# An mLSTM cell with a SwiGLU block: q of the second group transposed on VectorE, with its scores, state sums and attention one place later in the order

## The chip, the core and the metric

The kernel runs on one core of a Trainium2 chip. The metric is the device time of one execution in microseconds (us). The kernel before takes 506.29 us, the median of three runs (505.01 to 506.61).

A core has five engines, each with its own queue worked in program order: TensorE (PE; its weight loads are PEld), VectorE (DVE), ScalarE (ACT), GpSimd (POOL) and SyncE (SP), which here only issues DMAs. Engines wait for each other through semaphores. SBUF is the working memory; PSUM (8 banks) takes TensorE's results.

## The reference

Two stages. The first is a recurrence over 768 time steps for 4 batches and 8 heads of 40 features each, in float32:

```python
for t in range(S):
    m_new = np.maximum(f_gate[:, :, t] + m, i_gate[:, :, t])
    f_stab = np.exp(f_gate[:, :, t] + m - m_new)
    i_stab = np.exp(i_gate[:, :, t] - m_new)
    m = m_new
    C = f_stab * C + i_stab * einsum('bhd,bhe->bhde', vt, kt)
    n = f_stab * n + i_stab * kt
    h_tilde = einsum('bhde,bhe->bhd', C, qt)
    denom = np.maximum(np.abs(einsum('bhd,bhd->bh', n, qt)), 1.0)
    y[:, :, t] = sigmoid(o_gate[:, :, t]) * h_tilde / denom
```

The second takes y as x, 3072 tokens of 320 features, through a gated block of 1536 hidden units; its weights come in as 64-bit floats:

```python
g = x @ w_gate
out = (g * sigmoid(g) * (x @ w_val)) @ w_out
```

## The kernel before

**Groups.** The 768 steps are cut into six groups of 128 steps, numbered 0 to 5. The recurrence is done in closed form: within a half group of 64 steps by a 64x64 matrix of weighted scores for each head (`scores`, `weigh`, `attend_intra`), and across halves by a state C (`add`, `next_state`, `decayed`, `attend_inter`). `gather` adds the two parts of the attention and finds the divisor, `gate` puts the divisor into the output gate (on GpSimd), and `divide` makes x of it. P is 0 or 1 and names the half of the 32 pairs of batch and head (batches 0 and 1, or 2 and 3). `seam` transposes x to xT on TensorE, for the gated block.

**The pipeline.** While a group goes through the gated block, the attention of the next one is put between the pieces of that block. Group 0 is written out most carefully, as the weights arrive with it. Its hidden layer is 12 blocks of 128 hidden units, `hidden(0, m)`: 20 matmul instructions each (L808), a silu on ScalarE (L813) and a product on VectorE (L814). Then `project_all(0)` does the output products in 12 parts, 8 instructions each (L825); part m uses hidden block m. From group 1 on `gated` (L978) and `project_seven` (L879) do the same with fewer products.

**The weights.** They come as 64-bit floats in pieces (`piece_load`), and are made into 32-bit floats block by block. `scale(j)` does two ScalarE instructions (L249, L251), `join(j)` two on VectorE (L258, L259), and `rounded(j)` one (L266) on GpSimd, or on VectorE where `V` is given; `convert(j)` is the three in a row. Blocks 0 to 11 belong to the hidden layer, 12 to 17 to the output weights, two parts each: block 12 serves parts 0 and 1. Piece 7 holds blocks 10 and 11, piece 8 blocks 12 and 13. A piece has gate columns, loaded from SP's queue, and value columns, loaded from GpSimd's (L222).

**The order around the change.** It is written out by hand. `ahead[m]` and `first` are put behind block m's matmuls but ahead of its silu; `slots[m]` comes behind its product; `after[m]` behind part m of the output products. As every engine works its queue in this order, a place in these lists sets what stands ahead of what on each engine. In the kernel before:

- Group 1's k is loaded in slot 2, its q in slot 3 (`load_all`: two DMAs, L139), its v in slot 5. k is transposed on TensorE in slot 6 (`turn_one`, L378, copies on ScalarE by L156), q likewise in the middle of block 8 (`amid`).
- The weights of the scores, w_sb, are capped in slot 6 (L570), subtracted (L559) and put through exp (L577) in slot 7. GpSimd weighs v by them there (`weigh_values`, L422).
- The scores (L411) are in slot 8, with their weighing (L418), and a memset of q_sb on GpSimd ahead of them; the decays (L454) in slot 9, the state sums (L437) and state updates (L461) in slot 10.
- The attention of group 1's half P=0 (L478, L468) is in slot 11, that of P=1 behind part 1. The two divisions (L507) are behind parts 2 and 3, each with a pad copy of x on GpSimd (L510); the two seams (L543) behind parts 4 and 5.
- Group 2's q and k go another way: `load_squares` (L395) loads 32x32 squares, with 8 DMAs for each half, and `turn_squares` transposes the squares on VectorE (L401, two instructions).

**Banks.** PSUM has two rings of four banks here. One is for hidden blocks and output products ("gen"): each block takes two banks, so that block m+2 needs block m's silu and product done. The other ("cell") is for transposes, scores, sums and attention.

Of the kernel before, what the change touches and what calls it, by code (L numbers as in the profile page):

```python
# [13 lines left out]
AF = mybir.ActivationFunctionType  # L14
# [10 lines left out]
def kernel(  # L25
# [774 lines left out]
    def hidden(g, m, first=(), amid=()):  # L800
        ps = [bank("gv_ps", "gen") for _ in range(2)]
        x = xT(g)
        for kc in range(NKC):
            if kc == 3:
                for f in amid:
                    f()
# [285 lines left out]
    def load_all(dst, a, n, eng=nc.sync):  # L1092
        for P in range(2):
# [5 lines left out]
    on_vector = (9, 10)  # L1099
    ahead = {0: [], 1: [3], 2: [4], 3: [5], 4: [6], 5: [7], 6: [8], 7: [9], 8: [10], 9: [], 10: [], 11: []}  # L1100
# [3 lines left out]
        2: [run(late_maxima), run(M_store, G), run(load_all, k_sb, k, 1)],  # L1104
        3: [run(late_decay), run(weights_load, 1), run(load_all, q_sb, q, 1)],
        4: [run(nc.scalar.activation, step1, step1, AF.Exp), run(decay_rows), run(cap_table)],
# [136 lines left out]
```

## Time and profile before

| what | value |
|---|---|
| median of three runs | 506.29 us (505.01 to 506.61) |
| time of the profiled execution | 504.85 us |
| its span | 503.1 us |
| TensorE clock granted in its span | full (1.0) |
| group 0's hidden blocks | 25.96 to 86.72 us |
| group 0's output products | 88.73 to 119.0 us |
| DMA engines, mean busy share in the first eight slices of 12.6 us | 0.9 or more in six, then 0.8 and 0.7 |

The span goes from the first to the last instruction of the profiled execution; the time has 1.75 us more around it. The page of the profile gives the busy time of each engine and the chain of waits; the timelines give single instructions with start, length, engine, line, output and inputs. Times in a timeline are from the span's start. Two rows of the same engine can overlap a little, since an instruction's length includes its latency.

### The profile page before, as it was taken

The page shows a single profiled execution, that of the slowest core. Times are in us where ns is not written, and L with a number is a line of the kernel's source. Part 1 is how long each engine was busy: PE and PEld are TensorE (multiplying, and loading weights), DVE is VectorE, ACT ScalarE, POOL GpSimd, SP SyncE. Part 2 cuts the span into 40 slices and gives each one's busy share as a digit, 9 for nine tenths or more (in the row PEclk, how much of TensorE's full clock was granted, in tenths as well). Part 3 has the DMA queues.
Part 4 walks back from the last instruction along what each step waited for, and adds up shares of the span by engine and source line. Part 5 has one row for each costly group of instructions (what it writes and reads, how often), then busy time and mean ns, then how long its engine had stood idle before and what let it go on. Part 6 is the DMA issues. An engine that isn't in the chain of part 4 may idle for free.

```text
span 503.1 us, 14945 instructions
## 1 busy us (share of the span) xinstructions
PE 498.6 (99%) x6361; PEld 424.4 (84%) x6361; DVE 333.2 (66%) x542; ACT 209.2 (42%) x406; POOL 261.1 (52%) x292
## 2 busy tenths in 40 slices
PE   9999999999999999999999999999999999999997
PEld 4856555767889899888899888899888899988897
DVE  5889869889998587578376677467468464233421
ACT  4776784476262266323247312339311330223210
POOL 3753525458876925465723357643267650176710
PEclk9999999999999999999999999999999999999999
DMA  9999998797607982404991502991101100000001
GB/s 145 194 231 244 160 210 215 169 167 115 88 3 120 157 85 52 44 3 68 165 115 45 67 3 47 161 128 27 42 3 25 32 1 27 27 1 1 1 14 39
DMA packets 184938, 43.29 MB, mean 86 GB/s; under 512 B 173128, under 2 KB 180312, under 8 KB 184360
## 3 DMA queue, kind: packets, MB, share of 16 engines
q1 hardware_dynamic: 183396, 38.00, 48.0%
q0 software_dynamic: 1344, 4.28, 3.6%
q8 instruction: 50, 0.82, 0.7%
q14 instruction: 16, 0.13, 0.1%
q10 hardware_dynamic: 132, 0.07, 0.0%
HBM read 35.68 MB, written 4.01 MB: 79 GB/s over the span
## 4 chain that ended last, share of the span: by engine, by line
PE 97%; DVE 1%; ACT 1%; issue 0%; DVEq 0%
PE gv_x L978 26%; PE o_ps L879 22%; PE gv_y L978 21%; PE gv_ps L808 10%; PE o_ps L825 5%; PE inter L468 2%; PE sp L411 2%; PE intra L478 2%; PE o_ps L884 1%; PE add L437 1%; PE tp_kq L378 1%; PE sp L641 1%; PE tp_x L543 1%; PE wps L609 1%; PE burn L587 0%; PE wps L613 0%
## 5 line engine op out<-in xcount | busy, mean ns | idle before, releaser
L978 PE MATMUL gv_x<-xT,wgv_sb 64*128 64x256 f32 x720 | 89.1, 377 | 0.0
L978 PEld LDWEIGHTS gv_x<-xT,wgv_sb 64*128 64x128 f32 x720 | 69.3, 187 | 8.1 <-issue 0.2
L879 PE MATMUL o_ps<-wo_sb,h_sb 128*128 128x160 f32 x456 | 63.9, 300 | 0.0
L879 PEld LDWEIGHTS o_ps<-wo_sb,h_sb 128*128 128x128 f32 x456 | 62.3, 190 | 1.7 <-issue 1.7
L1026 ACT ACTIVATE h_sb<-gv_x 128x256 f32<-128x256 f32 x30 | 11.5, 384 | 116.3 <-PE gv_x L978 116.3
L808 PE MATMUL gv_ps<-xT,wgv_sb 64*128 64x512 f32 x240 | 53.8, 596 | 0.0
L808 PEld LDWEIGHTS gv_ps<-xT,wgv_sb 64*128 64x128 f32 x240 | 26.7, 187 | 22.6 <-issue 14.9
L978 PE MATMUL gv_y<-xT,wgv_sb 64*128 64x256 f32 x360 | 43.9, 376 | 0.0
L978 PE MATMUL gv_y<-q_sb,wgv_sb 64*128 64x256 f32 x360 | 43.9, 376 | 0.0
L422 POOL TENSOR_TENSOR vw_sb<-v_sb,w_sb 128x656 f32<-128x656 f32 x10 | 14.6, 1464 | 51.0 <-ACT w_sb L574 38.1
L978 PEld LDWEIGHTS gv_y<-xT,wgv_sb 64*128 64x128 f32 x360 | 34.9, 187 | 4.0
L978 PEld LDWEIGHTS gv_y<-q_sb,wgv_sb 64*128 64x128 f32 x360 | 34.9, 187 | 4.0
L574 ACT ACTIVATE w_sb<-w_sb,g_T 128x64 f32<-128x64 f32 x128 | 31.0, 334 | 0.0
L978 PE MATMUL gv_x<-q_sb,sw 64*128 64x256 f32 x240 | 30.9, 376 | 0.0
L879 PE MATMUL o_ps<-wT,S 128*128 128x160 f32 x216 | 30.2, 299 | 0.0
L879 PEld LDWEIGHTS o_ps<-wT,S 128*128 128x128 f32 x216 | 29.6, 190 | 0.0
L1019 POOL TENSOR_TENSOR tmp<-tmp 128x512 f32<-128x512 f32 x15 | 20.0, 1334 | 16.8 <-DVE tmp L1018 16.8
L999 POOL TENSOR_TENSOR h_sb<-x_sb 128x512 f32<-128x512 f32 x12 | 15.7, 1306 | 24.6 <-ACT x_sb L998 24.6
L999 POOL TENSOR_TENSOR h_sb<-tmp 128x512 f32<-128x512 f32 x13 | 16.5, 1269 | 21.5 <-ACT tmp L998 21.5
L846 POOL TENSOR_TENSOR S<-h_sb 128x256 f32<-128x256 f32 x30 | 22.6, 755 | 9.2 <-DVE h_sb L999 7.3
L1018 DVE TENSOR_TENSOR x_sb<-x_sb,gv_y 128x1024 f32<-128x1024 f32 x15 | 18.1, 1205 | 13.9 <-PE gv_y L978 11.6
L825 PE MATMUL o_ps<-wo_sb,h_sb 128*128 128x320 f32 x96 | 27.1, 438 | 0.0
(238 smaller groups left out, 1004.7 us busy)
## 6 DMA issues: line engine op xcount, KB each, us to landing
w_sb<-M_dram SPq DMA_DIRECT2D x8, 512.0 KB, 6.6
raw<-in_moe_w_out_dram SPq DMA_DIRECT2D x3, 1280.0 KB, 7.1
v_sb<-in_v_dram SPq DMA_DIRECT2D x11, 320.0 KB, 9.4
o_sb<-in_o_gate_dram SPq DMA_DIRECT2D x11, 320.0 KB, 5.0
k_sb<-in_k_dram SPq DMA_DIRECT2D x9, 320.0 KB, 7.3
x_sq<-k_sb SPq DMA_DIRECT2D x64, 40.0 KB, 2.8
q_sb<-in_q_dram SPq DMA_DIRECT2D x32, 64.0 KB, 3.7
out_dram<-tmp SPq DMA_DIRECT2D x24, 80.0 KB, 1.7
```

The source lines that it names most:

```text
L411: nc.tensor.matmul(sp[two][keys(n, P, i), a, :], lhsT=kT[feats(two), P * UA + a, half(i)], rhs=qT[feats(two), P * UA + a, half(i)], start= ...
L422: eng.tensor_tensor(vw_sb[:, heads(P)], v_sb[:, heads(P)], w_sb[:, heads(P), last].to_broadcast([128, UH, D1]), op=ALU.mult)
L574: nc.scalar.activation(w_sb[:, h], w_sb[:, h], AF.Exp, bias=g_T[:, n, h:h + 1], scale=-1.0)
L808: nc.tensor.matmul(ps[i], lhsT=wgv_sb[half(i), m, kc, :], rhs=x[half(i), kc, :], start=(kc == 0), stop=(kc == NKC - 1))
L825: nc.tensor.matmul(ps[u], lhsT=hid(g, m)[:, ts(u, L)], rhs=wo_sb[:, m, :], start=(m == 0), stop=(m == NFC - 1))
L846: eng.tensor_tensor(S1[:, k], lo[:, second_half], hi[:, second_half], op=ALU.add)
L879: nc.tensor.matmul(node[x][:, i], lhsT=lhs(k)[:, ts(i, L)], rhs=rhs(k), start=start and k == 0 and i == 0, stop=stop and k == KH - 1, skip ...
L978: nc.tensor.matmul(ps[:, i, cols], lhsT=lhs(c)[half(i)], rhs=rhs(c)[half(i)], start=start and c == 0, stop=stop and c == n - 1, skip_group ...
L999: (nc.vector if k == KH - 1 else nc.gpsimd).tensor_tensor(h_sb[:, 2 * k + 1], uw[:, 0], uw[:, 1], op=ALU.mult)
L1018: nc.vector.tensor_tensor(uw, uw, y, op=ALU.add)
L1019: nc.gpsimd.tensor_tensor(uw[:, :, second_half], uw[:, :, second_half], uw[:, :, first_half], op=ALU.add)
L1026: nc.scalar.activation(h[:, first_half], x[:, 0, first_half], AF.Silu)
```

## The change

Group 1's q is loaded as squares and transposed on VectorE, like that of the later groups, so that `amid` and the transposes of q on TensorE go. Its 16 square loads are in slots 2 and 4, where two loads stood in slot 3. Piece 7's two parts are loaded in slots 3 and 5 instead of 5 and 6. The caps and one subtraction move to slot 7, the second subtraction, exp and the weighing of v to slot 8, behind the conversion of block 10, which itself moves from ahead of block 8's silu to behind its product. The scores go from slot 8 to slot 10, the sums and state updates from slot 10 to slot 11, the attention of P=0 from slot 11 to behind part 0, that of P=1 from behind part 1 to behind part 2. The first sums of weights for group 1 (`weight_sums(0, V)`) move from behind part 10 to behind part 3, the transposes of group 2's q from behind part 4 to behind part 5. The memset of q_sb goes.

```diff
-    on_vector = (9, 10)
-    ahead = {..., 7: [9], 8: [10], 9: [], 10: [], 11: []}
+    on_vector = (9,)
+    ahead = {..., 7: [9], 8: [], 9: [], 10: [], 11: []}
     slots = {
...
-        2: [run(late_maxima), run(M_store, G), run(load_all, k_sb, k, 1)],
-        3: [run(late_decay), run(weights_load, 1), run(load_all, q_sb, q, 1)],
-        4: [..., run(decay_rows), run(cap_table)],
-        5: [run(piece_load, 7, parts=GATE), run(load_all, v_sb, v, 1), run(late_turns), run(decay)],
-        6: [run(piece_load, 7, parts=VALUE)] + [run(turn_one, P, k_sb, kT, (A, A)) for P in range(2)] + [run(weights_cap, 0), run(weights_cap, 1), run(piece_load, 8)],
-        7: [run(weights_sub, 1, 0), run(weights_sub, 1, 1), run(weights_exp, 0), run(weights_exp, 1), run(weigh_values, G, 0),
-            run(weigh_values, G, 1)],
-        8: [run(nc.gpsimd.memset, q_sb, 0.0), run(do_scores, 1), run(piece_load, 9), run(load_all, o_sb, o_gate, 1),
-            run(do_weigh, 0), run(do_weigh, 1)],
-        9: [run(join, 11), run(rounded, 11, V), run(do_decayed, 2)],
-        10: [run(do_add, 1), run(do_state, 2), run(rounded, 12), run(load_squares, q_sq, q, 2, (0,))],
-        11: [run(do_intra, 1, 0), run(do_inter, 1, 0), run(do_gather, 1, 0, False), run(piece_load, 10),
+        2: [run(late_maxima), run(M_store, G), run(load_all, k_sb, k, 1), run(load_squares, q_sq, q, 1, (0,))],
+        3: [run(late_decay), run(weights_load, 1), run(piece_load, 7, parts=GATE)],
+        4: [..., run(decay_rows), run(cap_table), run(load_squares, q_sq, q, 1, (1,))],
+        5: [run(piece_load, 7, parts=VALUE), run(load_all, v_sb, v, 1), run(late_turns), run(decay)],
+        6: [run(turn_one, P, k_sb, kT, (A, A)) for P in range(2)] + [run(piece_load, 8)],
+        7: [run(weights_cap, 0), run(weights_cap, 1), run(weights_sub, 1, 0)],
+        8: [run(convert, 10, V), run(weights_sub, 1, 1), run(weights_exp, 0), run(weights_exp, 1), run(turn_squares, q_sq, qT),
+            run(weigh_values, G, 0), run(weigh_values, G, 1), run(piece_load, 9), run(load_all, o_sb, o_gate, 1)],
+        9: [run(do_decayed, 2)],
+        10: [run(do_scores, 1), run(do_weigh, 0), run(scale, 12), run(join, 12), run(do_weigh, 1), run(rounded, 12),
+             run(load_squares, q_sq, q, 2, (0,))],
+        11: [run(do_add, 1), run(do_state, 2), run(piece_load, 10),
              run(load_squares, q_sq, q, 2, (1,))],
     }
-    amid = {8: [run(turn_one, P, q_sb, qT, (A, A)) for P in range(2)]}
...
-        first += {9: [run(scale, 11)], 10: [run(scale, 12), run(join, 12)], 11: [run(convert, 13)]}.get(m, [])
-        hidden(0, m, first, amid.get(m, ()))
+        first += {9: [run(convert, 11, V)], 11: [run(convert, 13)]}.get(m, [])
+        hidden(0, m, first)
...
     after = {
-        0: [run(convert, 14), run(sig, 0), run(sig, 1), run(do_gate, 0)],
-        1: [run(do_inter, 1, 1), run(do_intra, 1, 1), run(do_gather, 1, 1), run(weights_load, 2), run(load_all, v_sb, v, 2), run(load_all, k_sb, k, 2)],
-        2: [run(do_divide, 1, 0), run(convert, 15), run(early_squares, 0)],
-        3: [run(do_divide, 1, 1), run(weights_cap, 0)],
-        4: [run(seam, 1, 0, (A, A, A, A)), run(convert, 16), run(weights_cap, 1), run(turn_squares, q_sq, qT)],
-        5: [run(seam, 1, 1, (A, A, A, A)), run(convert, 17)],
+        0: [run(do_intra, 1, 0), run(do_inter, 1, 0), run(convert, 14), run(sig, 0), run(sig, 1), run(do_gather, 1, 0)],
+        2: [run(do_divide, 1, 0), run(do_inter, 1, 1), run(do_intra, 1, 1), run(do_gather, 1, 1), run(weights_load, 2),
+            run(load_all, v_sb, v, 2), run(load_all, k_sb, k, 2), run(convert, 15), run(early_squares, 0)],
+        3: [run(do_divide, 1, 1), run(weight_sums, 0, V)],
+        4: [run(seam, 1, 0, (A, A, A, A)), run(convert, 16), run(weights_cap, 0), run(weights_cap, 1)],
+        5: [run(seam, 1, 1, (A, A, A, A)), run(convert, 17), run(turn_squares, q_sq, qT)],
...
-        10: [run(do_decayed, 4), run(weight_sums, 0, V)],
+        10: [run(do_decayed, 4)],
...
     }
```

More of the change, by code (lines that the diff above doesn't have):

```diff
@@ L798, in hid, with hidden @@
         return h_sb[:, m, :]
-    def hidden(g, m, first=(), amid=()):
+    def hidden(g, m, first=()):
         ps = [bank("gv_ps", "gen") for _ in range(2)]
@@ L803, in hidden @@
         for kc in range(NKC):
-            if kc == 3:
-                for f in amid:
-                    f()
             for i in range(2):
@@ L1096 @@
     run = lambda f, *a, **b: (lambda: f(*a, **b))
-    on_vector = (9, 10)
-    ahead = {0: [], 1: [3], 2: [4], 3: [5], 4: [6], 5: [7], 6: [8], 7: [9], 8: [10], 9: [], 10: [], 11: []}
+    on_vector = (9,)
+    ahead = {0: [], 1: [3], 2: [4], 3: [5], 4: [6], 5: [7], 6: [8], 7: [9], 8: [], 9: [], 10: [], 11: []}
     slots = {
@@ L1115 @@
-        11: [run(do_intra, 1, 0), run(do_inter, 1, 0), run(do_gather, 1, 0, False), run(piece_load, 10),
+        2: [run(late_maxima), run(M_store, G), run(load_all, k_sb, k, 1), run(load_squares, q_sq, q, 1, (0,))],
+        3: [run(late_decay), run(weights_load, 1), run(piece_load, 7, parts=GATE)],
+        4: [run(nc.scalar.activation, step1, step1, AF.Exp), run(decay_rows), run(cap_table), run(load_squares, q_sq, q, 1, (1,))],
+        5: [run(piece_load, 7, parts=VALUE), run(load_all, v_sb, v, 1), run(late_turns), run(decay)],
```

1 line of the change is left out of this document (removed).

## The prediction

> **What bounds the kernel now.** First the page: its first part says how full each engine is, its chain of waits which work ended last.
>
> ```profile
> PE 498.6 (99%) x6361; PEld 424.4 (84%) x6361; DVE 333.2 (66%) x542; ACT 209.2 (42%) x406; POOL 261.1 (52%) x292
> ...
> PE 97%; DVE 1%; ACT 1%; issue 0%; DVEq 0%
> ```
>
> TensorE carries 97% of the chain and its granted clock is full, so a microsecond taken from TensorE's queue, or a wait put into it, moves the end by itself. Next the chain between 57 and 90 us (start, length, work), where the change acts.
>
> ```profile
> 58.25 0.99 PE tp_kq L378 x32
> 59.24 4.40 PE gv_ps L808 x20
> 63.63 0.59 ACT tmp L813
> ...
> 68.20 1.06 ACT qT L156 x2
> 69.26 0.04 issue
> 69.31 2.13 PE sp L411 x126
> 71.44 8.78 PE gv_ps L808 x40
> 80.22 2.01 PE add L437 x128
> 82.23 4.49 PE gv_ps L808 x20
> ```
>
> A hidden block costs TensorE 4.4 to 4.5 us. Between 63.63 and 69.31 the chain leaves it for ScalarE's copies of q, but TensorE works on: block 8 and, within it, 32 transposes of q. Last the timelines of VectorE, GpSimd, TensorE and the DMA queue, up to the seam at 105 us.
>
> ```profile
> 72.35 3.57 POOL L422 TENSOR_TENSOR vw_sb<-v_sb,w_sb 128x656 f32<-128x656 f32 x2 [12.26 <-ACT low L251]
> 73.05 1.71 DVE L266 CUSTOM_DVE_ANT_0 wgv_sb<-wgv_sb,low 128x1280 uint16<-128x1280 uint16 x1
> ...
> 98.17 1.31 POOL L501 TENSOR_TENSOR o_sb<-o_sb,den 128x640 f32<-128x640 f32 x1 [1.68 <-DVE den L496]
> 98.29 1.54 DVE L507 TENSOR_TENSOR x_sb<-o_sb,vw_sb 128x320 f32<-128x320 f32 x1
> ...
> 102.84 1.80 POOL L1128 MEMSET raw<- 128x2048 f32 x1
> 104.59 0.28 POOL L510 COPY x_sb<-x_sb 128x128 f32<-128x128 f32 x1
> ...
> 104.94 0.84 PE L543 MATMUL tp_x<-x_sq,x_sb 64*128 64x64 f32 x20
> ```
>
> Two things are to be seen. A VectorE instruction beside a GpSimd one can take far longer than alone: 1.71 us for a rounding that takes 0.83, 1.54 for a product that takes 0.43, the latter ending 0.35 us after GpSimd's gate. And the second seam starts 0.07 us after GpSimd's pad copy ends (104.87), with no idle before it: no slack there now.
>
> **Removed from TensorE.** The 32 transposes of q are like those of k: 0.99 us. From 63.63 to 69.31 are 5.68 us; less a block (4.40 to 4.49) and 0.99, 0.20 to 0.29 us of waiting for ScalarE's copies is left, 0.25. Together **-1.24 us**, all that the change can give, as every other TensorE instruction stays. ScalarE's four copies (2.03) and GpSimd's memset of q (1.80) go too, from engines that don't set the end.
>
> **Loads.** q's two loads (issues 5.56 us together) become 16. SP's 8 issues of such squares took 5.88 and 8.78 us. SP ends group 1's k at 47.68 and now waits for M until 51.04. Behind the change 8 squares go out to some 53.6, the weights' 1.1 to 54.7, and the gate part of piece 7 (blocks 10 and 11) behind them instead of at 57.96. With its 12.7 us to landing: 67.4, up to 69.4 if its issue takes 2 us as now. ScalarE reads it at 68.7 (below), so I cost this at 0; the cover is 0.7 us past that, the slack of block 10. The other 8 squares come next (to 60.6 or 63.5, landing at most 6.6 us later, before VectorE's transposes at 72.9), then v, 0.6 to 3.5 us later than now. v's first half lands at 72.2 now: 73 to 76. Piece 8 (blocks 12 and 13) is behind v and lands at 77.3 now: 78 to 81, where ScalarE reads it from 78 on and needs it by 80; 0.
>
> **VectorE after block 8.** Now laid in order. TensorE ends block 8 at 63.63 + 4.42 = 68.05; silu (0.60) 68.65. VectorE: product 7 to 64.93, caps 2.35, one subtraction 1.2, done at 68.4; product 8 at 69.35. ScalarE's scaling of block 10 ends at 70.15, join (0.49 + 0.82) and rounding (0.83) at 71.8; block 10 starts at 72.47, 0.65 us later: 0. Second subtraction 72.95, transposes (a pair takes 2.36 at 108.64) 75.3. They have no cost of their own, but block 11 now waits for what is behind them: join 11 (two instructions), rounding 11, product 9, some 3.0 us with gaps: 78.3 if undisturbed (ScalarE's two exps, scaling 11, table load and silu 9 end at 77.4). Block 11 wants product 9's banks when block 10 (76.9) and the scores (2.06) are done: 78.95. That is 0.65 us of slack. GpSimd's two weighings (3.57) and two decays (1.71) start with v, at 73 to 76, and lie beside just these instructions; now they start at 72.35. If each VectorE instruction loses what its kind lost beside GpSimd in this trace (rounding 0.88; second join instruction 1.24 against 0.82, so 0.42; first join instruction likewise 0.4), it is 1.7 less the slack: **+1.05 us**. From both sides: 0 if the weighings lie elsewhere; 2.2 if each of the three waits behind a whole weighing (1.46) or two decays (0.72 each).
>
> The Trainium skill (SBUF — State Buffer, the summary at its end) says that a VectorE instruction in a two-port mode, or with two SBUF inputs against a GpSimd instruction that reads SBUF, blocks until the other has finished. The 1.54 us row agrees, ending 0.35 us after the gate. By that rule whole blockings are due, and the term would be nearer the 2.2 end.
>
> **Scores, sums, attention.** Scores behind block 10 leave block 11 to cover the weighing of scores (2.47), join 12 and join 13 (1.31 each) and product 11 (0.69); the sums' 2.0 us on TensorE cover the rest. The first output part wants product 11's banks: 0 to 0.7, I take **+0.2 us**. State updates and decays took 3.2 us after the sums now; block 12's rounding must precede part 0, and attention P=0 has part 0 (2.23) and the sums' own 1.0 to cover them: 0.
>
> **The seam.** Let X be the end of attention P=0 on TensorE. Gathering took 3.64 us now (88.72 to 92.36), the gate 1.3, two divisions 0.85 alone: X+5.95. Only then VectorE gathers P=1, X+9.6 (its TensorE part ends at X+6.5); now nothing but a join stands between the two gatherings. GpSimd then has the gate (1.3), rounding 15 (1.55, behind join 15), the memset (1.8) and the pad copy (0.3), in this order: X+11.0, 12.6, 14.4, 14.7 at best; X+16.3 if join 15 loses 1.3 us to the gate and the rounding waits 0.3 for a division. TensorE has parts 1 to 5 (5 x 2.23), attention P=1 (2.0) and the first seam (0.77) before the second seam: X+13.9, and 0.6 of it needs no pad: X+14.5. The wait is 0.2 to 1.8 us; the divisions now lost 1.1 and 1.4 us to GpSimd at this very place, so I take **+1.6 us**. Moving the weight sums (four times 0.42) off the tail costs 0: VectorE has 13 us behind the seam.
>
> **Sum.** -1.24 + 1.05 + 0.2 + 1.6 = **+1.6 us**. The profiled execution has span 503.1 and time 504.85, 1.44 us below the median of the runs shown, 506.29. So it would be 506.5 beside its own time; on the median, **507.9 us**. 0.3% is 1.52 us, about what a measurement here tells from no change.
>
> **Rivals.** *Free of locks, and not slower* (-1.24 to +0.8 us, 505.0 to 507.1): GpSimd and VectorE do not meet. Block 11's wait falls below its 0.65 us of slack and the pad comes at X+14.7, a wait of 0.2: -1.24 + 0.2 = -1.0, 505.3 us. It decides where v's weighings start after 77 and join 15 is done by X+11. For it: most joins in this trace ran at full speed. Against it: v lands at 73 to 76 by SP's rows.
>
> *Late piece 7* (+2.0 to +3.8 us): the 16 square loads hold twice as many pieces as q's two loads (8192 runs of 128 and 32 bytes against 4096 of 160), in a stretch where the 16 DMA engines are busy throughout. If the gate part lands past 69.3, every microsecond more is one on block 10. At today's 70.7 it is 1.4 us; with the forecast's later waits (1.8) and -1.24, about +2.0, and at 72.5 it is +3.8: 508.3 to 510.1. Against it: it is issued some 3 us earlier.
>
> The Trainium skill (DMA: Bandwidth & Descriptors, Specifications) puts full rate at 512 bytes or more for each transfer; that speaks for this rival, and the profile's page has 173,128 of 184,938 packets under that size already.
>
> **Chances.** Forecast (both waits, +0.8 to +2.8 us, 507.1 to 509.1) 0.52, two thirds of it beyond 1.52 us; free of locks 0.27; late piece 0.17; something that I don't see, mostly a gain in TensorE's other waits, 0.04. So slower by over 0.3%: 0.52 x 0.65 + 0.17 x 0.95 = 0.50; within: 0.46; faster: 0.04, since 1.24 us is all the TensorE time there is to win. The range takes in -1.2 us and most of the late case: 505.1 to 510.1.
>
> **What would show it.** Right: no transposes of q on TensorE, the scores at 76.9 with no wait; TensorE idle before block 11 with VectorE's product 9 as releaser, and idle inside the second seam with GpSimd's pad copy (L510) as releaser; VectorE's joins of blocks 11 and 15 longer than 0.49 and 0.82. Wrong: block 10 waiting for its conversion (the late piece), or TensorE without idle at both places (free of locks). A wait in the last state sums at 119 us, where GpSimd's weighing now ends at 119.74, just in time, would show a cost of the moved weight sums that I left at 0.

## The result, and the profile after

The changed kernel took 506.82 us, the median of 22 runs (505.73 to 508.9), the kernel before 505.76 us in the 22 runs beside them (504.84 to 506.71): ratio 1.0025, 95% interval 1.0015 to 1.0036, some 1.3 us (1.06 between the medians). In a second comparison it was 1.0005 (0.9987 to 1.0024), where the kernel before against itself gave 1.0011 (0.9994 to 1.0029). So it is no faster and at most 0.4% slower. The best estimate lies within 0.3%, the case that the forecast had given 0.46; slower by more had been given 0.50. The profiled execution took 507.62 us, with a span of 505.9.

The page of the changed kernel, engines and chain of waits:

```profile
PE 498.8 (99%) x6329; PEld 421.3 (83%) x6329; DVE 334.2 (66%) x544; ACT 207.3 (41%) x402; POOL 259.2 (51%) x291
...
PE 89%; SPq 5%; DMA 2%; ACT 1%; issue 1%; DVE 1%; POOL 0%; DVEq 0%; POOLq 0%; ACTq 0%
```

TensorE lost its 32 transposes (6361 to 6329) and is busy for 99% of the span as before. Its share of the chain fell from 97% to 89%, but this is not lost time: the chain is followed back from the second seam through GpSimd's pad copy (108 to 80 us) and from the first hidden block through the load of the output gate (the first 25 us), and TensorE works beside most of both. What is lost is read in TensorE's own timeline (start, length, engine, line, operation, output and inputs, shapes, count, idle time before and its releaser):

```profile
60.39 1.16 PE L378 MATMUL tp_kq<-x_sq,k_sb 64*128 64x64 f32 x32
61.38 17.39 PE L805 MATMUL gv_ps<-xT,wgv_sb 64*128 64x512 f32 x80
78.70 2.10 PE L411 MATMUL sp<-qT,kT 40*64 40x64 f32 x128
80.76 5.06 PE L805 MATMUL gv_ps<-xT,wgv_sb 64*128 64x512 f32 x20
...
97.58 1.11 PE L478 MATMUL intra<-v_sb,w_sb 64*64 64x41 f32 x63
99.40 0.19 PE L478 MATMUL intra<-v_sb,w_sb 64*64 64x41 f32 x1 [0.71 <-issue]
99.52 4.57 PE L822 MATMUL o_ps<-wo_sb,h_sb 128*128 128x320 f32 x16
...
107.15 1.18 PE L543 MATMUL tp_x<-x_sq,x_sb 64*128 64x64 f32 x20
...
121.37 1.48 PE L437 MATMUL add<-vw_sb,k_sb 64*40 64x41 f32 x128
```

(Lines from L805 on are three lower than before.) Blocks 7 to 10 now run in one piece of 80 instructions, and the scores follow without a wait. Three places lose time: block 11 (80.76) takes 5.06 us where a block between other work takes 4.56 (the row below, of the kernel before); the second attention stops ahead of its last matmul, 0.71 us, marked issue, that is, for nothing that the profile shows; and the second seam takes 1.18 instead of 0.84.

```profile
82.16 4.56 PE L808 MATMUL gv_ps<-xT,wgv_sb 64*128 64x512 f32 x20
```

The timeline of VectorE and GpSimd at the first and the third place:

```profile
77.18 0.88 DVE L258 TENSOR_SCALAR wgv_sb<-top 128x640 uint32<-128x640 uint32 x1
77.67 2.26 POOL L454 TENSOR_TENSOR C<-C,dec 128x328 f32<-128x328 f32 x2
78.10 1.24 DVE L259 SCALAR_TENSOR_TENSOR wgv_sb<-top,wgv_sb 128x640 uint32<-128x640 uint32 x1
79.47 1.14 DVE L266 CUSTOM_DVE_ANT_0 wgv_sb<-wgv_sb,low 128x1280 uint16<-128x1280 uint16 x1
80.54 1.27 DVE L811 TENSOR_TENSOR h_sb<-tmp,gv_ps 128x512 f32<-128x512 f32 x2
...
102.28 1.76 DVE L259 SCALAR_TENSOR_TENSOR wo_sb<-top,wo_sb 128x640 uint32<-128x640 uint32 x1
104.17 1.67 POOL L266 TENSOR_TENSOR wo_sb<-wo_sb,low 128x640 int32<-128x640 int32 x1 [0.81 <-DMA w_sb<-M_dram]
105.79 1.80 POOL L1124 MEMSET raw<- 128x2048 f32 x1
107.54 0.39 POOL L510 COPY x_sb<-x_sb 128x128 f32<-128x128 f32 x1
```

Join and rounding 11 lie beside GpSimd and take 0.88, 1.24 and 1.14 us, against 0.49, 0.82 and 0.83 alone; product 9 (L811, the first of two, 0.67 us) ends 0.45 us after block 11's start, and block 11's second matmul starts right behind it, at 81.27. And the pad copy ends at 107.93, behind join 15 (1.76 us), rounding 15 and the memset, as the forecast had it. (The DMA named as releaser of rounding 15 is an inference of the profile; join 15 ends 0.13 us ahead of it, and in e5 it is marked issue.)

Each profiled execution can be cut into four stretches, us. A: when the first hidden block begins. B: from the first transpose of group 1's k to the end of block 11 and the state sums. C: from there to group 2's first state sum, the same TensorE work in all. D: the rest of the span. (Between A's point and B lie 31.99 to 33.08 us of work that the change leaves alone on TensorE. D is good to some 0.05 us, as spans are given to 0.1.)

| kernel | A | B | C | D | time |
|---|---|---|---|---|---|
| before, first profile | 25.85 | 28.57 | 32.34 | 384.11 | 504.85 |
| before, second (c_before) | 26.18 | 28.57 | 32.93 | 384.08 | 506.07 |
| changed, first | 28.40 | 27.37 | 33.61 | 384.53 | 507.62 |
| changed, second (c_after) | 26.34 | 27.50 | 33.89 | 384.62 | 506.42 |
| e1_pad_first | 26.94 | 27.10 | 33.50 | 385.15 | 506.84 |
| e2_join_early | 26.27 | 27.13 | 33.83 | 384.08 | 506.11 |
| e3_shift | 27.50 | 27.10 | 34.69 | 384.46 | 507.68 |
| e4_pad_shift | 27.16 | 27.50 | 35.32 | 384.30 | 508.18 |
| e5_align | 28.26 | 27.10 | 33.38 | 384.65 | 507.42 |
| e6_pad_align | 27.03 | 27.46 | 33.44 | 384.31 | 506.49 |
| e7_pad_join_align | 27.68 | 29.28 | 33.37 | 384.32 | 508.71 |
| e8_pad_caps_align | 27.09 | 27.71 | 32.65 | 386.14 | 507.47 |
| e9_order_only | 26.36 | 31.55 | 35.96 | 384.38 | 512.16 |
| b1_before_shift | 27.36 | 31.27 | 32.81 | 384.18 | 510.46 |

From before to changed: B -1.20 and -1.07, C +1.27 and +0.96, D +0.42 and +0.54; together +0.49 and +0.43 us. What the transposes gave in B, C took back. The stretch between A's point and B was 0.24 and 0.30 us shorter in the changed kernel; it spreads by 1.1 us over the executions, so this can't be put down to the change, but with it the changed kernel is only 0.2 us longer from the first hidden block to the end, in both pairs. A differs by up to 2.6 us between executions and is code that the change doesn't touch; 2.55 us of the 2.8 between the two first profiles are A.

### The profile page after: what moved, and what is told of

Same layout as the page of the kernel before. It is cut to its first block, busy times and chain, and to the rows that moved or that the text cites. A ratio compares the mean times of both kernels' runs of the same rounds, so it can differ in the third digit from the quotient of the medians.

```text
span 505.9 us, 14899 instructions
## 1 busy us (share of the span) xinstructions
PE 498.8 (99%) x6329; PEld 421.3 (83%) x6329; DVE 334.2 (66%) x544; ACT 207.3 (41%) x402; POOL 259.2 (51%) x291
## 4 chain that ended last, share of the span: by engine, by line
PE 89%; SPq 5%; DMA 2%; ACT 1%; issue 1%; DVE 1%; POOL 0%; DVEq 0%; POOLq 0%; ACTq 0%
PE gv_x L975 26%; PE o_ps L876 21%; PE gv_y L975 21%; PE gv_ps L805 10%; PE o_ps L822 3%; PE sp L411 2%; PE inter L468 2%; SPq L395 2%; PE intra L478 2%; DMA o_sb<-in_o_gate_dram 1%; PE o_ps L881 1%; SPq L139 1%; DMA w_sb<-M_dram 1%; PE add L437 1%; SPq L714 1%
## 5 line engine op out<-in xcount | busy, mean ns | idle before, releaser
L805 PE MATMUL gv_ps<-xT,wgv_sb 64*128 64x512 f32 x240 | 53.6, 597 | 0.0
L805 PEld LDWEIGHTS gv_ps<-xT,wgv_sb 64*128 64x128 f32 x240 | 24.2, 190 | 26.6 <-issue 23.3
```

The lines of the kernel that those rows point to most:

```text
L805: nc.tensor.matmul(ps[i], lhsT=wgv_sb[half(i), m, kc, :], rhs=x[half(i), kc, :], start=(kc == 0), stop=(kc == NKC - 1))
```

## The experiments

The theory after the result: block 11's wait and the pad copy are as forecast, and the 0.71 us are TensorE waiting for its own instructions. The page has a queue with 50 instruction transfers, 0.82 MB, 16 KB each; TensorE has 12,658 matmuls and weight loads and 121 semaphore and drain instructions on record, 12,779 in all, 256 for each transfer. Counting all of them from the trace's start, the gap stands ahead of number 2497, and the last transfer before it ran from 96.69 to 98.11. Rival: an accident of one execution, or a wait on another engine that the profile doesn't attribute.

**e1_pad_first** puts GpSimd's pad copy ahead of its memset:

```diff
-        2: [..., run(convert, 15), run(early_squares, 0)],
-        3: [run(do_divide, 1, 1), run(weight_sums, 0, V)],
+        2: [..., run(convert, 15)],
+        3: [run(do_divide, 1, 1), run(early_squares, 0), run(weight_sums, 0, V)],
```

> The changed kernel with one edit: GpSimd's pad copy of P=1 stands ahead of the memset of group 2's k squares. 'The stretch' is the time from the first transpose of group 1's k to the first state sum of group 2: 60.91 us in the kernel before, 60.98 in the changed one. Theory (three waits of TensorE took back the 1.24 us: block 11 behind VectorE's product 9, some 0.5; a gap of 0.71 in the attention of P=1; the second seam behind the pad copy, 0.34): the seam's wait goes, the stretch falls to 60.6, or by about 1 us if the 0.71 us gap is not there in this execution. Rival (the median's rise comes from a later start, as the profiled execution began its hidden blocks 2.5 us later): no change of the time beyond 0.3 us, and hidden blocks that begin at 28 us again.

507.34 us (before: 507.1), ratio 1.0008 (0.9992 to 1.0023). TensorE's timeline:

```profile
98.21 0.19 PE L478 MATMUL intra<-v_sb,w_sb 64*64 64x41 f32 x1 [0.93 <-issue]
```

The seam took 0.84, without a wait: the pad copy behind the memset is the seam's cause. The gap stayed, ahead of the same matmul, and the time is the kernel before's within the noise.

**e2_join_early** puts VectorE's conversion of block 11 right behind that of block 10:

```diff
-        8: [run(convert, 10, V), run(weights_sub, 1, 1), ...
+        8: [run(convert, 10, V), run(convert, 11, V), run(weights_sub, 1, 1), ...
-        first += {9: [run(convert, 11, V)], 11: [run(convert, 13)]}.get(m, [])
+        first += {11: [run(convert, 13)]}.get(m, [])
```

> The changed kernel with the conversion of block 11 (two instructions on ScalarE, three on VectorE) directly behind that of block 10, ahead of the second subtraction, the exps and the transposes of q. Theory (VectorE's conversion of block 11 is slowed by GpSimd's weighings and decays, and block 11 waits for the product behind it): conversion 11 takes 2.15 us on VectorE as alone, product 9 is done before the scores end, block 11 follows the scores with no wait, the stretch falls by some 0.5 us to 60.5. The scores may wait up to 1 us instead, as the transposes end 2.2 us later; then the stretch is unchanged. Rival (the wait at block 11 is ScalarE's silu 9 behind its table loads): block 11's wait stays 0.5 us.

506.18 us (before: 507.1), ratio 1.0001 (0.9981 to 1.0022). Join and rounding 11 took 2.14 us, as alone, but product 9 then waited for ScalarE's silu 9, as the rival had it:

```profile
79.16 1.28 DVE L811 TENSOR_TENSOR h_sb<-tmp,gv_ps 128x512 f32<-128x512 f32 x2 [0.75 <-ACT tmp L810]
```

Block 11 took 4.81 instead of 5.06, and that is no gain of this edit: e1, e3 and e5, which leave the order here alone, had 4.83, and the same B (27.10, here 27.13). C is 33.83, for the gap grew:

```profile
98.71 4.58 PE L822 MATMUL o_ps<-wo_sb,h_sb 128*128 128x320 f32 x16 [1.39 <-issue]
```

TensorE came to the same number, 2497, earlier and waited longer there. (It is one matmul further on, as this execution has one semaphore instruction less.)

**e3_shift** replaces three idle matmuls at the kernel's start by eleven short ones, 16 instructions more, and **e4_pad_shift** has both this and e1's edit:

```diff
-    burn(idle, 3, 256)
+    burn(idle, 11, 64)
```

> The changed kernel with 8 more small matmuls on TensorE near its start (11 of 64 columns in place of 3 of 256, whose result nobody uses), so that TensorE's instructions stand 16 places later in its stream. The gap of 0.71 us stands exactly 256 instructions behind the start of the attention of P=1, and a 16 KB instruction transfer began at that start (96.69 us, 1.41 us long). Theory (the gap is instruction loading: 256 instructions are used up in 2.0 us, before the next 256 are there): with the shift the gap is gone, but the second seam then waits for the pad copy by up to 0.71 us longer, 0.34 to 1.0, so that the time moves by less than 0.4 us. Rival (the gap is a wait for data or a semaphore): the gap is there as before.

> Both edits: 8 more small matmuls near TensorE's start, and the pad copy ahead of the memset. Theory (the instruction gap and the pad's wait hide each other, so that only both together give them back): the stretch falls by 0.7 to 1.1 us to 59.9 to 60.3, the time to that of the kernel before or up to 0.5 us below it. Rival (neither matters, the start does): the same time as the changed kernel, some 0.25% above the kernel before.

e3: 507.52 us, ratio 1.0015 (0.9999 to 1.0032); e4: 507.35, 1.0014 (0.9997 to 1.0031). TensorE's timelines, e3 first:

```profile
96.56 1.00 PE L478 MATMUL intra<-v_sb,w_sb 64*64 64x41 f32 x55
98.80 0.33 PE L478 MATMUL intra<-v_sb,w_sb 64*64 64x41 f32 x9 [1.23 <-issue]
```

```profile
99.80 0.33 PE L478 MATMUL intra<-v_sb,w_sb 64*64 64x41 f32 x9 [2.20 <-issue]
```

The gap did not go, so both expectations failed (e4's B and C together are 62.82); but it moved by eight matmuls, 16 instructions, to stand ahead of number 2497 again, though nothing near it was changed. A wait for data doesn't move with the idle matmuls at the start, so it is none; what goes by 256 instructions, as the transfers do, is their loading. Its size goes with the transfer: in the changed kernel, e1, e2, e3 and e4 the transfer ended at 98.11, 96.79, 97.17, 97.36 and 98.34, and TensorE resumed 1.29, 1.42, 1.54, 1.44 and 1.46 us later.

Why here: if each transfer brings the next 256 instructions, then between 61 and 101 us of the changed kernel's profile a transfer began only when TensorE was in the block of 256 instructions before the one it brings, 0.1 to 4.8 us after that block's first instruction. An output part uses 16 instructions in 2.25 us, a 128-matmul attention 256 in 2.0. In the changed kernel the second attention is exactly one such block (2241 to 2497), and its transfer had 2 us for what takes 1.4 and another 1.3. In the kernel before, two output parts fell between these numbers, which took 6.3 us (88.39 to 94.66); the transfer had ended at 90.30, and there was no gap.

**e5_align** adds 32 short idle matmuls at the start, 64 instructions, as many as the transposes had, so that everything behind lies against the borders of the loads as in the kernel before:

```diff
-    burn(idle, 4)
+    burn(idle, 32, 64)
...
-    burn(idle, 3, 256)
+    burn(idle, 7, 128)
```

> The changed kernel with 32 more small matmuls among the idle ones at its start (64 of TensorE's instructions, as many as the 32 transposes of q had), so that every later instruction lies where it lay in the kernel before against the borders of TensorE's 256-instruction loads. Theory (the attention's gap is instruction loading, and the second seam waits for GpSimd's pad copy whatever TensorE does): no gap of 0.3 us or more marked issue in group 1's attention; the pad copy ends as before, so the seam takes over the 0.71 us and waits 0.9 to 1.2 us; from the first transpose of group 1's k to the first state sum of group 2 some 61.0 us, and a time as the changed kernel's. Rival (the gap delays GpSimd's work as well, so that it is a loss of its own): the seam's wait stays at 0.2 to 0.5, the stretch falls to 60.3 and the time by 0.6 us. If the gap stands before the same matmul again, it isn't instruction loading at all.

506.86 us (before: 506.39), ratio 1.0004 (0.999 to 1.0018). TensorE's timeline:

```profile
80.80 4.83 PE L805 MATMUL gv_ps<-xT,wgv_sb 64*128 64x512 f32 x20
...
97.38 1.12 PE L478 MATMUL intra<-v_sb,w_sb 64*64 64x41 f32 x64
98.44 4.57 PE L822 MATMUL o_ps<-wo_sb,h_sb 128*128 128x320 f32 x16
...
106.06 0.71 PE L543 MATMUL tp_x<-x_sq,x_sb 64*128 64x64 f32 x16
...
107.57 0.34 PE L543 MATMUL tp_x<-x_sq,x_sb 64*128 64x64 f32 x4 [0.80 <-POOL x_sb L510]
```

No gap, and the seam takes 1.85 us instead of 0.84: a wait of 1.01, as the theory had it. This is the seam's price by itself. The changed kernel lost 0.89 (gap, to the next output part) and 0.34, together 1.23, so the gap cost it only some 0.2 beyond what the seam would have waited. This 0.2 is the part of the gap that also held VectorE's gathering of P=1 and, behind it, the pad copy; the row of the changed kernel:

```profile
99.63 1.55 DVE L491 TENSOR_TENSOR vw_sb<-vw_sb,intra 64x328 f32<-64x328 f32 x3 [0.28 <-PE intra L478]
```

In that respect the rival was right. The same wait is 0.55 in c_after and 1.22 in e3, where the seam waited 0.87 us on top of the gap. B and C together, 60.48, are 0.5 below the 61.0 expected: 0.27 of it in B (block 11 at 4.83; the first join instruction took 0.62 instead of 0.88), the rest what the gap had cost.

**e6_pad_align** has both e5's and e1's edit, **e7_pad_join_align** also e2's.

> As the one before, and the pad copy ahead of GpSimd's memset. Theory: neither gap nor wait in the seam; with the pad copy first the stretch was 60.60 with a gap of 0.93, so now 59.7 (59.5 to 60.0), 1.2 us below the kernel before's 60.91, and the time 0.5 to 1.2 us below that kernel's. Rival (something else takes the place: a wait for the output weights, or the gap elsewhere): the stretch stays above 60.3 and the time is that of the kernel before.

> As the one before, and VectorE's join of block 11 ahead of the second subtraction, the exponentials and the transposes of q. Theory: block 11 at 4.5 to 4.8 us instead of 5.06, the stretch at 59.2 to 59.7, the time 0.8 to 1.6 us below the kernel before. Rival (joining earlier moves the wait to the weighing of the scores or the state sums): the stretch is no shorter than that of the one before.

e6: 506.5 us, ratio 1.0 (0.9984 to 1.0015). e7: 507.37, 1.0014 (0.9989 to 1.0038). In e6 the seam took 0.84, but the 1.01 us came back: 0.41 in the first attention, by a gap marked 0.20 ahead of number 2241, and 0.66 in the last six output parts, by a new wait ahead of part 8, marked 0.39:

```profile
109.14 2.39 POOL L266 TENSOR_TENSOR wo_sb<-wo_sb,low 128x640 int32<-128x640 int32 x1 [1.35 <-DVE wo_sb L259]
...
111.58 4.84 PE L822 MATMUL o_ps<-wo_sb,h_sb 128*128 128x320 f32 x17 [0.39 <-POOL wo_sb L266]
```

Rounding 16 is next in line, held by the first seam's copies, scaling 16 and join 16 in turn; it is late in e4, e6 and e7, three of the four kernels that have the pad copy ahead and the caps where they were. So e6's rival was right: 60.90, no gain. The same wait is in the second profile of the kernel before, so that kernel has no slack there either (its first profile shows no wait):

```profile
111.41 8.88 PE L825 MATMUL o_ps<-wo_sb,h_sb 128*128 128x320 f32 x32 [0.50 <-POOL wo_sb L266]
```

In e7, too, the expectation failed: B is 1.8 us longer than in e6, mostly by a gap at another place, in block 11:

```profile
84.96 1.98 PE L805 MATMUL gv_ps<-xT,wgv_sb 64*128 64x512 f32 x6 [0.94 <-issue]
```

It stands ahead of number 1729, 768 before 2497. The transfer ran from 82.20 to 83.37, 3.7 us after TensorE had entered the block before (78.47); in e6 it had run at 78.04. The DMA engines were full then. The answer on DMA for 82.15 to 83.4 us of e7 (queue: packets, MB, share):

```profile
q1 hardware_dynamic: 1574, 0.25, 124.2%
q8 instruction: 1, 0.02, 5.8%
```

**e8_pad_caps_align** moves the caps of group 2's weights (L570), which lie beside rounding 16, behind the conversion of block 17, on top of e6 (the change had put both of them behind part 4, where one stood behind part 3):

```diff
-        4: [run(seam, 1, 0, (A, A, A, A)), run(convert, 16), run(weights_cap, 0), run(weights_cap, 1)],
-        5: [run(seam, 1, 1, (A, A, A, A)), run(convert, 17), run(turn_squares, q_sq, qT)],
+        4: [run(seam, 1, 0, (A, A, A, A)), run(convert, 16)],
+        5: [run(seam, 1, 1, (A, A, A, A)), run(convert, 17), run(weights_cap, 0), run(weights_cap, 1), run(turn_squares, q_sq, qT)],
```

> The changed kernel with the pad copy ahead of the memset, the instructions aligned as in the kernel before, and VectorE's two caps of group 2's weights moved behind the conversion of block 17, so that they no longer lie beside GpSimd's rounding of block 16 (2.39 us beside one of them, 1.55 without). Theory (with the seam's wait gone, the next bound is rounding 16, for which the output product waited 0.39 us): rounding 16 takes 1.5 to 1.7 us, no wait of 0.2 or more for the output weights, the stretch at 59.8 to 60.5, the time 0.2 to 0.8 us below the kernel before. Rival (rounding 16 is held by ScalarE's scaling, or the caps make rounding 17 or group 2's weights late): the wait stays or moves behind, and the time is the kernel before's within 0.1%.

509.26 us (before: 506.64), ratio 1.0055 (1.0037 to 1.0073). C is 32.65, the least of the changed kernels, and no output part waits. But the caps now make group 2's weights late, the rival's second half, and D is 1.8 us longer than in e6. The profiled execution is the quickest of six, 507.47; four of the others had a mean granted clock of 0.997 and took 509.2 to 509.9. The wait:

```profile
119.56 0.83 PE L437 MATMUL add<-vw_sb,k_sb 64*40 64x41 f32 x64
122.30 0.83 PE L437 MATMUL add<-vw_sb,k_sb 64*40 64x41 f32 x64 [1.92 <-POOL vw_sb L422]
```

**e9_order_only** keeps the change's order but loads q in rows and transposes it on TensorE in block 8, so that VectorE has no transposes:

```diff
-            ..., run(load_squares, q_sq, q, 1, (0,))],
+            ..., run(load_all, q_sb, q, 1)],
...
-        8: [..., run(weights_exp, 1), run(turn_squares, q_sq, qT),
-            run(weigh_values, G, 0), run(weigh_values, G, 1), ...
+        8: [..., run(weights_exp, 1),
+            run(weigh_values, G, 0), run(weigh_values, G, 1), run(nc.gpsimd.memset, q_sb, 0.0), ...
+    amid = {8: [run(turn_one, P, q_sb, qT, (A, A)) for P in range(2)]}
```

> The change's order of everything, but with q still loaded in rows and transposed by TensorE within block 8 (32 transposes, ScalarE's four copies, GpSimd's memset of q behind its two weighings), so VectorE has no transposes of q here. Theory (what the change gives is TensorE's 1.24 us, what it costs is the order; the transposes cost VectorE's queue only the 0.3 to 0.5 us at block 11): 32 transposes of 0.99 to 1.3 us and a wait of 0.2 to 0.3 for ScalarE's copies come back, block 11 takes 4.5 to 4.7 instead of 5.06, no gap in the attention (its instructions lie where they lay before), the seam waits 0.8 to 1.2 us; the stretch 61.3 to 62.0 and the time 0.3 to 1.0 us above the changed kernel's. Rival (VectorE's transposes themselves are what costs): the stretch is 60.5 or less and the time at or below the kernel before's.

510.71 us (before: 506.64), ratio 1.0091 (1.0056 to 1.0125). Both were wrong by far: B and C take 67.51. The timeline of GpSimd, VectorE and TensorE:

```profile
73.80 2.82 POOL L422 TENSOR_TENSOR vw_sb<-v_sb,w_sb 128x656 f32<-128x656 f32 x2 [14.50 <-ACT w_sb L577]
75.95 2.75 DVE L258 TENSOR_SCALAR wgv_sb<-top 128x640 uint32<-128x640 uint32 x1 [1.81 <-ACT top L249]
76.56 1.80 POOL L1096 MEMSET q_sb<- 128x2048 f32 x1
78.74 1.23 DVE L259 SCALAR_TENSOR_TENSOR wgv_sb<-top,wgv_sb 128x640 uint32<-128x640 uint32 x1
81.40 6.73 PE L808 MATMUL gv_ps<-xT,wgv_sb 64*128 64x512 f32 x20 [1.43 <-DVE wgv_sb L266]
...
96.63 0.44 PE L468 MATMUL inter<-C,qT 40*64 40x41 f32 x16 [2.38 <-issue]
```

Without the transposes join 11 starts within the second weighing, and its first instruction, 0.49 us alone, takes 2.75: it ends 0.34 us after the memset, which began while it stood there. In the changed kernel join 11 starts at 77.18, behind the transposes and most of the weighings. The kernel has the memset at another place than the change would, so it is no clean half of the change; it shows what GpSimd beside join 11 can cost. Then TensorE's clock fell for 3.4 us and block 11 took 6.73 us, and a gap came ahead of number 2241, 256 before 2497, with a transfer from 94.11 to 95.17, 4.3 us after the block before was entered, and TensorE back 1.46 us after its end.

**b1_before_shift** is the kernel before with 24 more idle instructions at its start, meant to put a border on the first of group 1's state sums:

```diff
-    burn(idle, 3, 256)
+    burn(idle, 15, 64)
```

> The kernel before, with nothing but 12 more small matmuls among the idle ones at its start (24 instructions of TensorE), so that a border of its 256-instruction loads falls on the first of the 128 matmuls of group 1's state sums, which use up 256 instructions in 2.0 us. Theory: a gap of 0.9 to 1.7 us marked issue at the end of these sums (or at the first matmul of block 11), though nothing of the change is in this kernel; group 1's stretch 0.9 to 1.7 us longer than 60.91 unless a later wait takes some of it back, and a time 0.3 to 1.5 us above the kernel before. Rival (the gap comes from the order of the change): no gap there, the same stretch and the same time.

508.98 us (before: 506.39), ratio 1.0048 (1.0025 to 1.0071), but not for the reason given: the sums had no gap. An earlier wait had held TensorE ahead of them, and the transfer was under way at 84.82 when they began at 85.00. ScalarE's and TensorE's rows:

```profile
74.78 0.78 ACT L249 ACTIVATE top<-raw 128x640 f32<-128x640 f32 x1 [2.20 <-DMA raw<-in_moe_w_gate_dram]
...
80.01 5.06 PE L808 MATMUL gv_ps<-xT,wgv_sb 64*128 64x512 f32 x20 [1.73 <-DVE wgv_sb L266]
```

This is the rival *Late piece 7*, in the kernel before: M's store and load came later (SP goes on at 53.0 instead of 51.0, of which 1.5 us are the later start of the hidden blocks), and piece 7 stands behind them. It is no accident of one execution: all ten took 507.9 us or more. So twelve short idle matmuls at the start cost more than the whole change, and why is open. For the mechanism of the gap the run is inconclusive: that one can be made in the kernel before is not shown.

**c_after and c_before** are the two kernels unaltered, with a second profile each.

> The changed kernel unaltered, for a second profiled execution and a second comparison. Theory (the gap is fixed by the instruction's index, its size by when the load starts): a gap of 0.5 to 2.2 us marked issue before the same matmul near the end of group 1's second attention, the sum of gap and seam wait 0.9 to 1.2 us if the gap is below 1; the stretch from the first transpose of group 1's k to the first state sum of group 2 at 60.4 to 61.5; the first hidden block beginning at 26 to 28.4 us. The time 0.3 to 1.5 us above the kernel before. Rival (the gap was an accident of one execution): no gap.

> The kernel before unaltered, for a second profiled execution. Theory (the early start of its first hidden block, 25.85 us, was this one execution's luck, since ten kernels alike up to there began at 26.3 to 28.4): it begins at 26 to 28 this time, the stretch stays at 60.6 to 61.3, no gap marked issue above 0.3 us in it, and the time is that of the kernel before within 0.2%. Rival (the changed kernels begin later because of something in the change): it begins below 26.2 again.

506.99 us, ratio 1.0005 (0.9987 to 1.0024), and 507.0, 1.0011 (0.9994 to 1.0029), beside 506.64. TensorE's timeline of c_after:

```profile
79.09 5.06 PE L805 MATMUL gv_ps<-xT,wgv_sb 64*128 64x512 f32 x20
...
98.01 0.19 PE L478 MATMUL intra<-v_sb,w_sb 64*64 64x41 f32 x1 [0.98 <-issue]
...
105.75 1.18 PE L543 MATMUL tp_x<-x_sq,x_sb 64*128 64x64 f32 x20
```

The same three places with the same block 11 and seam; the gap is ahead of the same matmul. Gap (1.17 to the next output part) and seam make 1.51, above the 1.2 expected. The first block begins at 26.34 and 26.18, so the 28.40 was that one execution's. But 26.18 is below 26.2, the sign that c_before's rival had named: both profiles of the kernel before begin earlier than all eleven with the change's order (26.27 to 28.40). No instruction ahead of that point differs but for idle matmuls, and b1, which has nothing of the change, begins at 27.36; so a later start as a cost of the change is neither shown nor excluded.

No version is shown to beat the kernel before: the best, e2 and e6, are at 1.0001 and 1.0 of it. (e2's nine executions with a mean granted clock of 0.999 or 1.0 have a median of 506.11, against 507.09 of such executions of the kernel before; its three others, at 508.4 to 510.1, take that back.)

## Why the prediction was right, and where it was off

It put the likeliest time at +1.6 us; the comparisons gave +1.3 and +0.3, the profiles +0.5. The mechanism held: TensorE gains in front, VectorE's join beside GpSimd takes a part back at block 11, and GpSimd's pad copy would take 1.01 us at the second seam, were it not for a gap that the forecast didn't have. That +1.6 lies near the first +1.3 is partly luck: four of its terms were off by 0.2 to 0.6 us, two waits were missing, and the terms as profiled add up to +0.5. By its steps:

- **Removed, -1.24: too small.** B fell by 1.20 and 1.07 with a wait of 0.50 at block 11 in it, so 1.6 to 1.7 were removed. 0.99 are the transposes. The waiting for ScalarE's copies was not 0.25 but some 0.6: from block 7's start to block 9's the kernel before took 12.30 us, of which two blocks in a row (8.66, from 80 instructions in 17.32), the transposes (0.99) and scores without a wait (2.06) make 11.71. I took 4.40 to 4.49 off for block 8, the length of a block that stands alone, and looked for waiting only up to 69.31, though the scores waited on behind it: 2.58 us before, 2.10 after.

```profile
69.49 2.58 PE L411 MATMUL sp<-qT,kT 40*64 40x64 f32 x128
```

(the second profile of the kernel before).
- **Loads, 0: right.** Scaling 10 began at 70.71 without waiting; both profiles of the kernel before waited for piece 7 there (0.51 and 0.32 us), b1 2.20. No changed kernel waited for it: late piece 7 didn't happen. What was off is the second eight issues of squares, 12.17 us and not 5.88 to 8.78, which put v's issue at 70.46; v still landed in time for the first weighing at 74.64.
- **Block 11, +1.05: right in kind, measured 0.50** in both profiles of the changed kernel, and 0.27 in e1, e3 and e5 with the same order there. Join and rounding lost 0.39, 0.42 and 0.31 us, 1.1 together, not 1.7, as they start behind most of the weighings, and the slack was about as forecast. e2 shows that moving them doesn't remove the wait, for silu 9 is next; e9 is the upper end: losses of 2.26, 0.41 and 0.31 us, 3.0 together, about the 2.9 less the slack that made my upper bound of 2.2, and product 9 ended 1.9 us after the scores.

The Trainium skill (SBUF — State Buffer, the summary at its end), cited in the prediction, has whichever of VectorE's and GpSimd's instructions issues second blocked until the first ends, under the conditions named there. The runs agree: 1.81 us for c_after's second join instruction, ending 0.7 after a weighing, and 2.75 us in e9. But in e9 the join instruction had begun 0.61 us ahead of the memset and still ended 0.34 after it, which the rule as put there doesn't cover. What the rule doesn't give is how much of GpSimd's work lies there.

- **First output part, +0.2: measured 0.** Part 0 followed the sums in every changed kernel.
- **The second seam, +1.6: measured 1.01** without a gap (e5). The place and the cause were exact: e1, and e6 without a gap of TensorE near it, removed the wait by the order on GpSimd alone. Join 15 lost 0.94 us, not 1.3, and its rounding did not wait for a division.
- **Not foreseen: the gap** (0.89 and 1.17 us), which took the place of most of the seam's wait (0.34 left) and cost 0.2 to 0.5 beyond it, about as much as VectorE's gathering waited for it (0.28 and 0.55). The step that failed is the count of TensorE's own instructions: I costed what is issued, not that 64 fewer instructions shift all that follows against the borders of its loads.
- **Not foreseen: the tail, +0.42 and +0.54.** 0.4 of each is one wait in group 2's attention (144 us and 142 us), of which 0.21 and 0.22 are marked as idle. The rows of the changed kernel's first profile, GpSimd, VectorE and TensorE:

```profile
138.82 1.45 POOL L1016 TENSOR_TENSOR x_sb<-x_sb 128x512 f32<-128x512 f32 x1
139.06 1.49 DVE L953 TENSOR_TENSOR wgv_sb<-wgv_sb 128x256 f32<-128x256 f32 x1
...
143.84 1.14 PE L478 MATMUL intra<-v_sb,w_sb 64*64 64x41 f32 x64 [0.21 <-issue]
```

L953 takes 0.94 in e2, e4, e6 and e7, where it begins 0.6 us ahead of GpSimd's instruction and not 0.2 behind it, and there the wait is absent, as in the kernel before; e1, e3 and e9 have both. That the weighing of scores, starting 0.35 us later, is what shifted it, is read from the order of rows and wasn't tried by itself.

The time alone doesn't decide between the cases: 506.82 lies in the range given to *Free of locks* (505.0 to 507.1) and just below that of the forecast's own case. The traces do: *Free of locks* was wrong in both its halves, by 0.50 and 1.01 us, and the removed part, 0.4 larger, is what brought the sum nearer to 0.

Why the first comparison gave 1.3 us and the profiles 0.5 is explained in part. Six of the changed kernel's 22 executions there had a mean granted clock of 0.995 to 0.997, and their median is 508.2 us; the other 16, at 0.999 or 1.0, had 506.5, 0.8 above the kernel before. The 1.7 us between the two are what 3.4 us at half clock lose. For the kernel before's 22 executions the clocks are not on record, but for the profiled one (1.0); where they are, 8 of 103 of its executions had such a clock, and 8 of 33 of the changed kernel's. Whether the change makes this likelier wasn't tried. The second comparison, 0.3, and the kernel before's own 0.6 against itself say that the rest can be the spread of these measurements.

## What to carry to other kernels

When work moves off the bounding engine, follow the chain of the other engines to the next place where that engine needs them: here a join slowed beside GpSimd and a memset ahead of a 0.3 us copy were worth 1.01 us at the seam (e5), as much as the 32 transposes. A length taken from an instruction group that stands alone is too long for one in a row, and a wait can sit inside the next group. Where many short instructions follow each other (256 in 2 us), look in the trace for idle time marked issue, and count the instructions to see whether it keeps to one number; do not tune such a gap by an edit that only moves it. And look at the granted clock of every execution before a difference of 0.3% is put down to an edit.

## What the runs showed of the hardware

**Instruction loads can hold TensorE.** The gaps stood ahead of numbers 1729, 2241 and 2497 of its recorded instructions, multiples of 256 apart, in eight of the profiled executions (and, with 0.20 us, ahead of 2241 in e6), and 16 more instructions at the start moved a gap by 16. TensorE resumed 1.2 to 1.6 us after the end of a 16 KB transfer that took 1.0 to 1.4. If each of the 50 transfers brings the next 256 instructions, none in the 14 profiles began more than 302 instructions ahead of its block. The transfer of the changed kernel's second profile, in the answer on DMA for 95.2 to 96.6 us; TensorE resumed at 98.01:

```profile
q1 hardware_dynamic: 1513, 0.16, 94.5%
q8 instruction: 1, 0.02, 5.8%
```

The Trainium skill (Runtime: NRT & Kernel Launch, Instruction fetch mechanics) says that instructions come in blocks of 256 and that crossing a border is mostly hidden. The blocks agree; the cost doesn't for bursts of short matmuls: 0.71 to 2.38 us here, and the measurement decides.

**The clock can fall for some microseconds.** In e9 the granted clock was 0.50 from 82 to 84 us, and in the changed kernel's first profile 0.53 from 26 to 28, each after an idle time of some 1.4 us; e1 and e5, with 1.34 and 2.24 us of idle at that second place, and b1, with 1.73 ahead of block 10, kept 1.0 throughout. At half clock the lost shares of e9's windows (0.03, 0.50 and 0.32 of 2 us each) make 3.4 us; those of the changed kernel (0.47 and 0.38) the same. The Trainium skill (TensorE: Matmul & The Clock Gate, Part 1: The HAM clock gate) has the clock set by TensorE's activity in windows of 3.4 us that run freely; the length agrees, and where an idle time lies against such a window could tell e5 from the others, which no run here shows. The page's table asks for a whole idle window; 1.4 us is less, and the measurement decides. Windows of e9 (busy time and count of five engines, clock, DMA share, GB/s):

```profile
80.00:82.00 2.00, 0.60 (x3) 0.39 (x4) 1.89 (x3) 1.46 (x2) 0.57 (x1) 0.97 1.05 385
82.00:84.00 2.00, 2.00 (x7) 1.26 (x7) 2.00 (x4) 0.00 (x0) 0.00 (x0) 0.50 1.19 201
```

**The start varies.** Fourteen profiled executions with the same work up to the first hidden block, but for a few idle matmuls, began it between 25.85 and 28.40 us, for a good part by when the output gate's load landed: ScalarE's sigmoid waited 0.31 us for it in the kernel before's first profile, 0.46 in e2, 1.81 in e1, 1.88 in the changed kernel's first and 2.66 in e5. In the changed kernel's first profile the half clock from 26.1 us on adds some 1.1 us to the 28.40. The spread is more than the whole effect of the change, so single executions can't be compared by their ends.
